# Thresholded attention and a gated MLP in one kernel: MLP jobs three steps sooner, one more threshold on ScalarE in five pairs, another order of the tail

## The chip, the core and the metric

The kernel runs on one core of one Trainium2 chip, as one launch. The metric is the device time in microseconds; the kernel before took 480.41 us as the median of three runs (479.06 to 481.51). Engines are named as the profile names them: PE is TensorE's matmul, PEld its weight load, DVE VectorE, ACT ScalarE, POOL GpSimd, SP the engine whose queue issues most DMAs. "L586" is line 586 of the kernel before.

## What is computed

Attention over 8 batches of 8 heads, 576 rows of 64, in which only scores within tau of a row's maximum count, and then a gated MLP with a spatial product over the 576 rows:

```python
scores = (1 / np.sqrt(64)) * np.matmul(q, k.transpose(0, 1, 3, 2))      # q, k, v: (8, 8, 576, 64)
thresh = np.max(scores, axis=-1, keepdims=True) - tau                   # tau = 0.02
scores = np.where(scores >= thresh, scores, -1e9)
attn = np.exp(scores - np.max(scores, axis=-1, keepdims=True))
attn = attn / (np.sum(attn, axis=-1, keepdims=True) + 1e-9)
x = np.matmul(attn, v)                           # heads side by side: (8, 576, 512)
h = np.maximum(x @ w_in, 0)                      # w_in: (512, 1024)
u, v = h[..., :512], h[..., 512:]
v_n = (v - mean(v)) / np.sqrt(var(v) + 1e-6)     # over the last axis
v_s = np.einsum('ts,bsd->btd', w_spatial, v_n) + b_spatial[None, :, None]
out = (u * v_s) @ w_out                          # (8, 576, 512)
```

## The kernel before, in words

**Pairs, chunks, steps.** Two heads make a pair i, of which there are 32, four to a batch. The 576 rows of a pair are cut into chunks c = 0 to 3 of 128 rows; the 64 rows left over of an even pair and of the odd pair after it make one chunk 4, which is done at the start of the odd pair. So an even pair has the steps 0, 1, 2, 3 and an odd one 4, 0, 1, 2, 3: 144 steps g = 0 to 143, nine to two pairs, eighteen to a batch. The order of all queues is written out by hand: each step writes its instructions in turn, and each engine runs its own in that order.

**One step** (`step`, L574). PE multiplies the scores of both heads into a tile s of three PSUM banks (`scores`, L545 for the last 64 columns, L550 for the first 512); there are two such tiles, so the scores of step g+2 wait until the exponentials of step g have read theirs. DVE takes the maximum (L586). On most chunks ACT then computes e = exp(s - max), one instruction a head (L609), and DVE, one step later in `mask` (L558), sets what is below exp(-tau) to nothing and writes p in bf16 (L567, a SCALAR_TENSOR_TENSOR over 1152 columns). On the chunks for which `on_act` is true the threshold is ACT's: DVE turns the negative maximum into tau - max (L590), ACT runs Prelu with a slope of 1e30 below zero (L603, in the place of L609) and one Exp over 1152 columns that writes p (L605); `mask` then has no DVE work. Before, these are chunks 2 and 4. After chunk 1 and chunk 3, `mask` issues on SP a DMA transpose of two chunks of p into pT (L571), after chunk 4 one of the rest (L562).

**Jobs in a step.** `fs` lists what a step does beside its own scores: the transposes of the next pair's q and k on PE with copies by ACT (qk_main at chunks 0 and 2, qk_rem at chunk 1), the product with v (pv, L289 and L294; its divide is DVE's, L301 and L303), and the jobs of the MLP. The list is sorted so that jobs that ACT evicts come first and jobs that DVE evicts after them, the products of the left-over rows (pv_rest) last. The first two are put before the maximum; ACT's evictions of these go ahead of the step's exponentials. Further jobs are put after the exponentials, and their ACT evictions are held until the next step. All jobs but the scores rotate through two PSUM banks (tiles f), so the third job of a step waits for the eviction of the first.

**MLP jobs.** For each batch b there are five v jobs (moe_v: x times the right half of w_in, L418; ACT's Relu L428, two steps later its Square L442, and a chain on POOL that writes the normalised vn, L436 to L448; the fifth, L403 and L406, has the rest rows and the last rows of the output of the batch before), five u jobs (moe_u, L460 and L465, ACT's Relu L475 or L477), five s jobs (moe_s, the spatial product, L490 and L495, whose gating product with u is DVE's, L504 or L507), and four o jobs (moe_o, L519, ACT's copy L524 and an output DMA). They are placed by three names: batch b's round begins at step LAG + 18 b, the letters of ORDER are put one to a step from there on, and s and o belong to the batch before. With 19 letters the last o shares its step with the first letter of the next round. Jobs whose step would lie beyond 143 go into `last` and are run in the tail.

**Other work with a step number.** `x_jobs` transposes x on PE for the first seven pairs; later pairs use DMA transposes. `ws_pe` transposes w_spatial on PE, five jobs. `chores` holds loads of the weights on SP and casts on POOL. The loads of q, k and v go through `sends`, one a step, behind `mask`. POOL reorders q, k and v for the pairs to come (shape_qk at chunk 2, shape_v at chunk 0).

**The head and the tail.** The first pair's transposes go to the banks of the score tiles (`first`). After step 143 the score tiles are given up and the other banks are six more; `run` writes jobs one after the other: those in `last`, the last products with v, the transposes of x on PE (x_pe), the s jobs of batch 6, and then `last_gmlp` for batch 7, which starts with its v products (L643).

Of the kernel before, what the change touches and what calls it, by code (L numbers as in the profile page):

```python
# [17 lines left out]
def kernel(  # L18
# [21 lines left out]
    NPAIR = B * H // 2  # L40
# [267 lines left out]
    def pv(i, part):  # L308

        b, hp = divmod(i, HP)  # L310
        hold = {}

        def mm():
            t = hold["t"] = bank()
            for k in range(2):
                weigh(t, 130 * k, pts[i, part][:, k], v_ring[i % 4])

        def ev():
            if part == 0:
                xns[i] = xp.tile([P, 4, P], BF16, name="xn")  # L320
            xn = xns[i]
            divide(hold["t"], [(slice(0, P), 0, 4,
                                xn[:, 2 * part:2 * part + 2, :].rearrange(
                                    "p c (h d) -> p (c h) d", h=2))])
            if part == 1:
                if hp == 0:
                    xts[b] = xtp.tile([P, 4, 640], BF16, name="xT")
                if i in x_on_pe:
                    return
                sends.append(lambda: nc.sync.dma_start_transpose(  # L330
                    out=xts[b][:, hp, 0:512].rearrange("p (c s) -> p c s", s=P),
                    in_=xn.rearrange("p c d -> p (c d)")))
        return "dve", mm, ev
# [217 lines left out]
                                 rhs=qks[n][hs, 1, 0:512], start=True, stop=True)  # L551
        return view(s, 0, [[960, 2], [1, S]])

    def on_act(c):

        return c in (2, 4)

    def mask():  # L558
        i, c, e = unmasked.pop()
        if c == 4:  # L560
            dst = pts[i // 2] = ptr_ring[i // 2 % 2]
            nc.sync.dma_start_transpose(out=dst, in_=pr_ring[i // 2 % 2])  # L562
            return
        pt = p_ring[2 * (i % 2) + c // 2]
        if not on_act(c):
            ef = e.rearrange("p h s -> p (h s)")
            nc.vector.scalar_tensor_tensor(out=pt[:, c % 2, :], in0=ef, scalar=ctau, in1=ef,  # L567
                                           op0=ALU.is_ge, op1=ALU.mult)
        if c % 2:
            dst = pts[i, c // 2] = ptp.tile([P, 2, 9, P], BF16, name="pT")  # L570
            nc.sync.dma_start_transpose(out=dst.rearrange("p c b s -> p (c b) s"),  # L571
                                        in_=pt.rearrange("p c s -> p (c s)"))

    def step(i, c, fs):  # L574

        s = scores(i, c)
        while held:
            held.pop(0)()


        for kind, mm, ev in fs[:2]:
            mm()
            if kind == "act":
                ev()
        nm = small.tile([P, 2], F32, name="negm")
        nc.vector.tensor_reduce(out=nm, in_=s, axis=AX.X, op=ALU.max, negate=True)  # L586

        by = scale if c == 4 else 1.0
        if on_act(c):
            nc.vector.tensor_scalar(out=nm, in0=nm, scalar1=by, scalar2=float(tau),  # L590
                                    op0=ALU.mult, op1=ALU.add)
        for kind, mm, ev in fs[:2]:
            if kind == "dve":
                ev()
        due = [f for n, f in later if n <= 0]
        later[:] = [(n - 1, f) for n, f in later if n > 0]
        for f in due:
            f()
        e = ep.tile([P, 2, S], F32, name="e")
        if on_act(c):  # L600

            for h in range(2):
                nc.scalar.activation(out=e[:, h, :], in_=s[:, h, :], func=ACT.Prelu,  # L603
                                     bias=nm[:, h:h + 1], scale=by, alpha=1e30)
            nc.scalar.activation(out=pr_ring[i // 2 % 2] if c == 4 else p_ring[2 * (i % 2) + c // 2][:, c % 2],  # L605
                                 in_=e.rearrange("p h s -> p (h s)"), func=ACT.Exp)
        else:
            for h in range(2):
                nc.scalar.activation(out=e[:, h, :], in_=s[:, h, :], func=ACT.Exp,  # L609
                                     bias=nm[:, h:h + 1])  # L610
        ready = sends[:]
        sends.clear()
        if unmasked:
            mask()
        for f in ready:
            f()
        unmasked.append((i, c, e))
        for kind, mm, ev in fs[2:]:
            mm()
            if kind == "dve":  # L620
                ev()
            else:
                held.append(ev)
# [115 lines left out]
    chores[13] = (load_w_in, 3)  # L739
    for gs_, f in (((4, 5, 6, 17), shape_w_in),  # L740
                   ((20, 25, 30), load_ws), ((24, 26, 29, 31, 34), shape_ws),
                   ((36, 41, 46, 51), load_w_o), ((39, 44, 49, 54), shape_w_o)):
        chores.update({g: (f, j) for j, g in enumerate(gs_)})

    LAG = 26
    ORDER = "vsvsvsvssuvuouououo"
    jobs, last = {}, []
    for b in range(B):  # L750
        n = dict.fromkeys("vuso", 0)
# [10 lines left out]
    Z = B - 1  # L762
# [1 line left out]
    for g, j in x_jobs:  # L764
        jobs.setdefault(g, []).append((x_pe, j))
    for j in range(5):
        jobs.setdefault((29, 33, 34, 42, 44)[j], []).append((ws_pe, j))
    with tc.manual_schedule():
        for w in (0, 1):
            for f in load(0, 1, w, (nc.sync, nc.scalar)[w]):  # L770
                f()
        make_identity(nc, identf)
        clear()
        nc.vector.memset(ntau, -float(tau))
        nc.vector.memset(mhalf, -0.5)
        nc.scalar.activation(out=ctau, in_=ntau, func=ACT.Exp)
        nc.vector.tensor_copy(out=identb, in_=identf)
        for w in (0, 1):
            for f in load(1, 1, w):
                f()  # L780
        for f in load(0, 2, 2):
            f()
        for j in range(3):
            load_w_in(j)
        for _ in range(14):
            nc.tensor.transpose(out=ps_f.tile([P, 512], F32, name="f")[:, 0:P], in_=identf,
                                identity=identf)
        shape_first()
        first()
        shape_qk(1)  # L790
        queue = []
        for g, (i, c) in enumerate(steps):
            if c == 2 and i + 2 < NPAIR:
                shape_qk(i + 2)
            if c == 0:
                shape_v(i)
            if c == 0 and i % 2 and i + 3 < NPAIR or g == 0:
                for w in range(3):
                    queue.extend(load(i + (3 if g else 2), 2, w))
            if g in chores:  # L800
                chores[g][0](chores[g][1])
            fs, small_ones = [], []
            if i + 1 < NPAIR and c < 3:
                fs.append(qk_rem(i + 1) if c == 1 else qk_main(i + 1, c // 2))
            if i and c == (2 if i % 2 else 3):
                fs.append(pv(i - 1, 0))
            if i > 1 and c == 4:
                fs.append(pv(i - 2, 1))
            if i % 2 and c == 3:
                fs.append(pv(i - 1, 1))  # L810
            if i % 2 and i > 1 and c == 1:
                small_ones = [pv_rest(i // 2 - 1)]
                fs += small_ones
            fs += [f(*a) for f, *a in jobs.get(g, [])]
            fs.sort(key=lambda f: (f[0] == "dve", f in small_ones))
            sends += queue[:1 if g > 3 else 2]
            del queue[:1 if g > 3 else 2]
            step(i, c, fs)

        def run(*fs):  # L820
            for f in fs:
                f[1]()
                f[2]()
                for f in sends:
                    f()
                sends.clear()
        while held:
            held.pop(0)()
        mask()
        inner.close()  # L830
        wide.append(ctx.enter_context(tc.tile_pool(name="ps_t", bufs=6, space=PSUM,
                                                  reuse_waits="tile")))
        for _, f in later:
            f()
        last = [f(b, j) for f, b, j in last]
        run(last[0], pv_rest(NPAIR // 2 - 1), *last[1:3], x_pe(NPAIR - 2), *last[3:6],
            pv(NPAIR - 1, 0), *last[6:], pv(NPAIR - 1, 1), moe_s(Z - 1, 0), moe_s(Z - 1, 1),
            x_pe(NPAIR - 1, True), *[moe_s(Z - 1, j) for j in range(2, 5)])
        rest = last_gmlp(Z)
        next(rest)  # L840
        run(moe_u(Z, 0), moe_u(Z, 1))
        next(rest)
        run(*[moe_u(Z, j) for j in range(2, 5)], *[moe_o(Z - 1, j) for j in range(4)])
        next(rest)
        next(rest, None)
# [35 lines left out]
```

## Time and profile before, and how to read it

| what | us |
|---|---|
| median of three runs | 480.41 |
| the profiled execution | 480.41 |
| its span, first to last instruction | 478.6 |
| scores of step 5, 23, 45 start at | 19.27, 68.26, 134.53 |
| a round of 18 steps from step 45 to 135 | 55.24, 55.67, 55.35, 55.21, 55.21 |
| last maximum (step 143) starts at | 437.70 |
| v products of batch 7 (L643) start at | 452.82 |

| one instruction | count | mean us |
|---|---|---|
| L586 DVE maximum | 144 | 1.353 |
| L567 DVE threshold | 96 | 1.444 |
| L590 DVE tau - max | 48 | 0.305 (median 0.170) |
| L609 ACT Exp of one head | 192 | 0.741 |
| L603 ACT Prelu of one head | 96 | 0.738 |
| L605 ACT Exp to p, both heads | 48 | 1.165 |

The page gives for each engine the busy time and its share of the span. The table by stretch gives the same for a piece of the span: its bounds and length, then busy us and instructions of PE, PEld, DVE, ACT and POOL, TensorE's granted clock, the share of the DMA engines, and GB/s. The timeline lists start, duration, engine, line, operation, tiles, and in brackets how long the engine sat idle before and what released it. The chain that ended last is followed back from the last instruction, and shows start, duration and line. Instructions that follow each other on DVE and ACT overlap by some 0.08 us in their records, so I count from start to start where a sum matters.

### The profile page before, as it was taken

The page shows a single profiled execution, that of the slowest core. Times are in us where ns is not written, and L with a number is a line of the kernel's source. Part 1 is how long each engine was busy: PE and PEld are TensorE (multiplying, and loading weights), DVE is VectorE, ACT ScalarE, POOL GpSimd, SP SyncE. Part 2 cuts the span into 40 slices and gives each one's busy share as a digit, 9 for nine tenths or more (in the row PEclk, how much of TensorE's full clock was granted, in tenths as well). Part 3 has the DMA queues.
Part 4 walks back from the last instruction along what each step waited for, and adds up shares of the span by engine and source line. Part 5 has one row for each costly group of instructions (what it writes and reads, how often), then busy time and mean ns, then how long its engine had stood idle before and what let it go on. Part 6 is the DMA issues. An engine that isn't in the chain of part 4 may idle for free.

```text
span 478.6 us, 9894 instructions
## 1 busy us (share of the span) xinstructions
PE 448.3 (94%) x3664; PEld 238.3 (50%) x3664; DVE 418.0 (87%) x563; ACT 382.2 (80%) x666; POOL 229.1 (48%) x403
## 2 busy tenths in 40 slices
PE   7788888889899999999999999999999999999995
PEld 4344444454554555554555545555554545545542
DVE  4999999989889997999889898899889998898573
ACT  4778777998879798788979898798978889797251
POOL 3462544784337553474427652475436743253021
PEclk9899999999999999999999999999999999999999
DMA  7999999979999799898988999997996999766523
GB/s 225 255 185 199 223 236 197 214 159 204 179 191 194 172 212 223 189 170 183 192 197 202 182 200 191 223 190 156 222 227 170 195 173 218 138 113 120 149 82 117
DMA packets 231120, 89.38 MB, mean 187 GB/s; under 512 B 200608, under 2 KB 225312, under 8 KB 231072
## 3 DMA queue, kind: packets, MB, share of 16 engines
q1 hardware_dynamic: 230416, 87.86, 87.2%
q8 instruction: 29, 0.48, 0.4%
q0 software_dynamic: 160, 0.52, 0.3%
q10 hardware_dynamic: 496, 0.36, 0.2%
q14 instruction: 19, 0.16, 0.1%
HBM read 33.31 MB, written 9.44 MB: 89 GB/s over the span
## 4 chain that ended last, share of the span: by engine, by line
PE 48%; DVE 23%; ACT 19%; issue 6%; DMA 2%; SPq 1%; POOL 0%; POOLq 0%; ACTq 0%; DVEq 0%
PE s L550 14%; DVE negm L586 10%; DVE p L567 8%; PE f L245 5%; ACT e L609 5%; PE s L545 4%; ACT e L603 4%; PE f L294 4%; PE f L519 4%; PE f L460 3%; ACT p L605 2%; ACT vrel L428 2%; PE f L490 2%; PE f L289 2%; ACT sq L442 1%
## 5 line engine op out<-in xcount | busy, mean ns | idle before, releaser
L586 DVE TENSOR_REDUCE negm<-s 128x2 f32<-128x1152 f32 x144 | 194.8, 1353 | 26.1 <-PE s L550 25.3
L550 PE MATMUL s<-qkT 64*128 64x512 f32 (+1 forms) x640 | 162.9, 639 | 0.0
L567 DVE SCALAR_TENSOR_TENSOR p<-e,ctau 128x1152 bf16<-128x1152 f32 x96 | 138.6, 1444 | 1.3 <-ACT e L609 1.2
L609 ACT ACTIVATE e<-s,negm 128x576 f32<-128x576 f32 x192 | 131.8, 741 | 7.1 <-DVE negm L586 6.8
L603 ACT ACTIVATE e<-s,negm 128x576 f32<-128x576 f32 x96 | 65.9, 738 | 20.9 <-DVE negm L590 11.6
L545 PE MATMUL s<-kd,qkT 128*128 128x128 f32 (+1 forms) x320 | 64.4, 304 | 15.6 <-ACT e L609 10.5
L268 POOL COPY kd<-qkT 64x64 f32<-64x64 f32 x62 | 31.7, 512 | 91.2 <-ACT qkT L263 89.4
L545 PEld LDWEIGHTS s<-kd,qkT 128*128 128x128 f32 (+1 forms) x320 | 44.4, 180 | 34.7 <-ACT e L609 20.2
L550 PEld LDWEIGHTS s<-qkT 64*128 64x128 f32 (+1 forms) x640 | 42.1, 174 | 18.3 <-issue 3.0
L436 POOL TENSOR_SCALAR nmean<-sm 128x1 f32<-128x1 f32 (+1 forms) x35 | 15.3, 437 | 69.7 <-ACT vrel L428 64.3
L294 PEld LDWEIGHTS <-pT 128*128 128x128 bf16 x1024 | 41.8, 97 | 7.3 <-issue 4.8
L294 PE MATMUL f<-v,pT 128*128 128x65 bf16 x992 | 44.9, 194 | 0.0
L136 POOL COPY qn<-ql 128x640 f32<-128x640 f32 x31 | 34.7, 1120 | 21.2 <-DMA ql<-in_k_dram 15.1
L605 ACT ACTIVATE p<-e 128x1152 bf16<-128x1152 f32 x32 | 37.3, 1165 | 1.0
L252 ACT COPY qkT<-f 128x512 f32<-128x512 f32 x31 | 18.2, 587 | 16.4 <-PE f L245 16.4
L490 PE MATMUL f<-wsT,vn 128*128 128x512 bf16 x125 | 31.1, 379 | 0.0
L448 POOL TENSOR_SCALAR vn<-vrel,rs,nm 128x512 bf16<-128x512 f32 (+1 forms) x34 | 28.7, 844 | 3.7
L289 PE MATMUL f<-v,pT 128*128 128x130 bf16 x124 | 27.2, 219 | 3.5 <-ACT qkT L252 1.6
L460 PE MATMUL f<-xT,w_in 128*128 128x512 bf16 x112 | 28.7, 380 | 0.9 <-DVE xn L303 0.8
L418 PE MATMUL f<-w_in,xT 128*128 128x512 bf16 x112 | 28.8, 380 | 0.0
L303 DVE TENSOR_TENSOR xn<-f,r 128x256 bf16<-128x256 f32 x62 | 26.3, 425 | 2.1
L428 ACT ACTIVATE vrel<-f 128x512 f32<-128x512 f32 (+1 forms) x34 | 20.1, 592 | 7.6 <-PE f L418 5.2
(165 smaller groups left out, 638.7 us busy)
## 6 DMA issues: line engine op xcount, KB each, us to landing
vl<-in_v_dram SPq DMA_DIRECT2D x16, 512.0 KB, 4.4
ql<-in_q_dram SPq DMA_DIRECT2D x15, 512.0 KB, 4.6
kl<-in_k_dram SPq DMA_DIRECT2D x15, 512.0 KB, 4.5
out_dram<-o SPq DMA_DIRECT2D x20, 256.0 KB, 3.4
uT<-in_moe_w_in_dram SPq DMA_DIRECT2D x3, 512.0 KB, 6.6
uT<-in_moe_w_spatial_dram SPq DMA_DIRECT2D x2, 576.0 KB, 5.0
vl<-in_v_dram SPq DMA_DIRECT2D x16, 64.0 KB, 4.1
pT<-p SPq DMA_TRANSPOSE x64, 5.5
```

Of the source, the lines that this page charges most:

```text
L136: nc.gpsimd.tensor_copy(out=t, in_=ld_ring[i // 2 % 2][w][:, 2 * (i % 2):2 * (i % 2) + 2].rearrange("p h c d -> p c h d"))
L289: nc.tensor.matmul(out=t[:, at:at + 130], lhsT=pt[:, 4, :], rhs=vt[:, 4:6, :].rearrange("p b d -> p (b d)"), start=True, stop=False)
L294: nc.tensor.matmul(out=t[:, at + 65 * h:at + 65 * h + 65], lhsT=pt[:, 5 * h + j, :], rhs=vt[:, 6 * h + j, :], start=False, stop=(h == 1 an ...
L460: nc.tensor.matmul(out=t, lhsT=w_in[:, m, f * P:(f + 1) * P], rhs=xts[b][:, m, 0:512], start=(m == 0), stop=(m == 3))
L490: nc.tensor.matmul(out=t, lhsT=vn[:, c, f * P:(f + 1) * P], rhs=wsT[:, c, 0:512], start=(c == 0), stop=(c == 4))
L545: nc.tensor.matmul(out=view(s[rows], 512, [[448, 2], [1, 64]]), lhsT=qks[n][:, 0, m], rhs=kd_ring[n % 2], start=True, stop=True)
L550: nc.tensor.matmul(out=s[rows, 1024 * h:1024 * h + 512], lhsT=qks[n][hs, 0, m], rhs=qks[n][hs, 1, 0:512], start=True, stop=True)
L567: nc.vector.scalar_tensor_tensor(out=pt[:, c % 2, :], in0=ef, scalar=ctau, in1=ef, op0=ALU.is_ge, op1=ALU.mult)
L586: nc.vector.tensor_reduce(out=nm, in_=s, axis=AX.X, op=ALU.max, negate=True)
L603: nc.scalar.activation(out=e[:, h, :], in_=s[:, h, :], func=ACT.Prelu, bias=nm[:, h:h + 1], scale=by, alpha=1e30)
L605: nc.scalar.activation(out=pr_ring[i // 2 % 2] if c == 4 else p_ring[2 * (i % 2) + c // 2][:, c % 2], in_=e.rearrange("p h s -> p (h s)"), ...
L609: nc.scalar.activation(out=e[:, h, :], in_=s[:, h, :], func=ACT.Exp, bias=nm[:, h:h + 1])
```

## The change

Four edits. `on_act` also holds for chunk 0 of pairs 1 to 5 (steps 5, 9, 14, 18 and 23). LAG goes from 26 to 23 and ORDER changes: the v jobs keep their steps, but for the fifth, which is two sooner; the u jobs come three or four steps sooner, the s jobs four to six and the o jobs three. The transposes of w_spatial are spread over other steps, and w_out is loaded and cast one to four steps sooner. In the tail `last` now holds six jobs instead of nine, and two of batch 6's s jobs go between the two last products with v, a third before x_pe.

```diff
-    def on_act(c):
-
-        return c in (2, 4)
+    def on_act(i, c):
+
+        return c in (2, 4) or c == 0 and 0 < i < 6
...
-                   ((36, 41, 46, 51), load_w_o), ((39, 44, 49, 54), shape_w_o)):
+                   ((35, 39, 43, 47), load_w_o), ((38, 42, 46, 50), shape_w_o)):
...
-    LAG = 26
-    ORDER = "vsvsvsvssuvuouououo"
+    LAG = 23
+    ORDER = "sssvsvsvuvuvouououo"
...
-        jobs.setdefault((29, 33, 34, 42, 44)[j], []).append((ws_pe, j))
+        jobs.setdefault((27, 29, 35, 37, 39)[j], []).append((ws_pe, j))
...
         run(last[0], pv_rest(NPAIR // 2 - 1), *last[1:3], x_pe(NPAIR - 2), *last[3:6],
-            pv(NPAIR - 1, 0), *last[6:], pv(NPAIR - 1, 1), moe_s(Z - 1, 0), moe_s(Z - 1, 1),
-            x_pe(NPAIR - 1, True), *[moe_s(Z - 1, j) for j in range(2, 5)])
+            pv(NPAIR - 1, 0), moe_s(Z - 1, 0), moe_s(Z - 1, 1), pv(NPAIR - 1, 1),
+            moe_s(Z - 1, 2), x_pe(NPAIR - 1, True), moe_s(Z - 1, 3), moe_s(Z - 1, 4))
+        assert len(last) == 6, len(last)
```

The calls of `on_act` pass the pair as well. Instructions change in number only by the five thresholds: five L567 fewer, five L590 and five L605 more, ten L603 in the place of ten L609.

## The prediction

> **What bounds the kernel now.** I read the page's busy shares first, then the same engines by stretch, then the waits, then the chain at the end. The profiled execution took 480.41 us for a span of 478.6 us. That is also the median of the three runs, so I work in its times and need no correction between the two; 1.8 us lie outside the span.
>
> ```profile
> PE 448.3 (94%) x3664; PEld 238.3 (50%) x3664; DVE 418.0 (87%) x563; ACT 382.2 (80%) x666; POOL 229.1 (48%) x403
> ```
>
> One share for the whole span says little, because the kernel has a head, a steady middle and a tail. The table by stretch (columns: us, then busy us of each engine) parts them. Steps are counted by the starts of the L545 matmuls: step 14 starts at 43.15, 23 at 68.26, 45 at 134.53, and from there each round of 18 steps takes 55.2 to 55.7 us, up to step 135 at 411.21.
>
> ```profile
> 45.50:70.60 25.10, 20.14 (x178) 10.91 (x177) 24.70 (x31) 19.08 (x30) 9.67 (x14) 1.00 1.00 209
> 70.60:96.10 25.50, 22.60 (x190) 12.01 (x189) 24.10 (x30) 22.30 (x41) 16.11 (x28) 1.00 1.08 207
> 96.10:123.20 27.10, 24.65 (x208) 13.40 (x207) 24.19 (x30) 24.70 (x45) 17.50 (x33) 1.00 0.91 185
> 300.80:356.00 55.20, 54.48 (x453) 28.82 (x450) 49.36 (x63) 47.42 (x85) 28.82 (x49) 1.00 0.92 196
> ```
>
> ```profile
> 437.70:474.00 36.30, 36.02 (x296) 18.37 (x292) 23.00 (x54) 16.19 (x31) 5.00 (x6) 1.00 0.40 107
> ```
>
> The reader is to see three regimes. Before gMLP begins (first row) DVE is busy 24.70 of 25.10 us; PE has 5 us to spare, ACT 6. In a steady round (fourth row) it is PE: 54.48 of 55.20, and its gaps add to 0.7 us. In the tail PE is busy 36.02 of 36.30. So work taken off DVE pays in the head, work taken off PE pays in the tail, and in the middle only the order can matter. The timeline of DVE in the head carries the first claim; no row has an idle mark:
>
> ```profile
> 68.64 0.17 DVE L590 TENSOR_SCALAR negm<-negm 128x2 f32<-128x2 f32 x1
> 68.72 0.17 DVE L301 RECIPROCAL r<-f 128x4 f32<-128x4 f32 x1
> 68.93 0.42 DVE L303 TENSOR_TENSOR xn<-f,r 128x256 bf16<-128x256 f32 x1
> 69.27 1.41 DVE L567 SCALAR_TENSOR_TENSOR p<-e,ctau 128x1152 bf16<-128x1152 f32 x1
> 70.60 2.76 DVE L586 TENSOR_REDUCE negm<-s 128x2 f32<-128x1152 f32 x2
> ```
>
> And the chain that ended last, at the seam of loop and tail, goes over from DVE to PE:
>
> ```profile
> 436.46 1.33 DVE p L567
> 437.78 1.27 DVE negm L586
> 439.05 0.10 DVE r L301
> ...
> 439.66 1.04 PE f L460 x4
> 440.69 0.86 PE t L519 x4
> ```
>
> **Term 1, the threshold in pairs 1 to 5 (steps 5, 9, 14, 18, 23).** Each loses one L567 on DVE, from start to start 69.27 to 70.60 = 1.33 us, and gains one L590, 68.64 to 68.72 = 0.08 (its mean is 0.305, its worst 1.12 where GpSimd copies beside it). DVE saves 5 x 1.25 = 6.25 us. ACT gains one L605 of 1.165 us each, some 1.1 from start to start; the two Prelu replace two Exp at 738 against 741 ns. For the row 45.50:70.60, with two such pairs, DVE falls from 24.70 to 22.2 and ACT rises from 19.08 to 21.3, PE stays at 20.1: DVE stays the longest, so up to 2.5 us per nine steps may go. What is late next: Prelu now waits for reduction and L590 where Exp waited for the reduction alone; the exponentials of the next step queue behind L605 on ACT, and PE's scores two steps on wait for them. SP is the other: between 45.3 and 70.6 its issues add to 23.6 us, the pT transposes among them at 2.7 to 5.0 us each, with both rings of loads between them. If those durations are fixed, nine steps can't go below 23.6, a gain of 1.5 instead of 2.5. Pair 1 saves less: its L567 at 25.59 follows 0.98 us in which DVE waited for PE. Bounds 0 to -6.25; I take **-4.0**, nearer to the DVE row, because SP's shortest pT issue (2.7) shows that the long ones stretch with the queue.
>
> The Trainium skill, ScalarE: Activation LUTs, section Table sets, says that a switch between functions of different sets costs a table load, about 2.66 us. Were Prelu and Exp in different sets, five pairs would pay two switches each, an estimate of 27 us more, and the sum would be 501 us. Page part 5 by shape has one load in the whole execution, although chunks 2 and 4 alternate the two functions 48 times, so I charge nothing:
>
> ```profile
> L776 ACT ACT_TABLE_LOAD x1 | 1.3, 1283 | 2.0 <-issue 2.0
> ```
>
> **Term 2, the tail.** With LAG 23 the last round fits 13 jobs into the loop, not 10: the fifth v job, one u and one o leave the tail. There they cost PE 0.9 (four L403/L406 pairs, 437.77 to 438.66), 0.87 and 0.86 (439.66 to 440.69 to 441.56 in the chain): -2.6. The loop's last five steps lose three s jobs too: two L504 and one L507, 0.6 + 0.6 + 0.33 us on DVE, which the chain shows binding there until 439.66. ACT gets a u, the v job and its copies instead, and has a 2.5 us idle stretch before 435.69 to take them. I count half of 1.5: -0.7. The order of the tail: pv(31,1) needs the transpose that was issued at 441.97 and landed at 446.55, while pv(31,1) ran at 447.02. Counting PE forward from the last scores (435.33) with three jobs fewer and s0, s1 put ahead of it, it comes up at 445.3; with the loop's end 0.7 to 1.5 earlier the landing comes to 445.1 to 445.9. The two meet, so the wait is 0 to 0.6. The divide behind it (0.6 on DVE) lies beside s2 (1.08 on PE). Each job that moves takes its output DMA along (one for o, one for the fifth v, 0.54 us of SP) and the v job its chain on GpSimd, which is busy 12.5 of the loop's last 29 us; both have room. Bounds: -4.1 with all of 1.5, and -1.0 where the wait is 0.6 and ACT's new work holds the loop's end back by 1; I take **-3.3**.
>
> **Term 3, what the loop takes in.** Up to step 44 it now also runs s0, s1, s2 of batch 0 (steps 41 to 43): 3 x 1.08 us on PE, 3 x 0.6 on DVE. PE's gaps between 68 and 134 add to 6.6 us, so a part lies in them; PE's scores, evictions and weights' transposes of steps 27 to 43 come to some 47.4 us of PE, 46 of DVE, 48 of ACT for 51 elapsed. Bounds 0 to +3.3, I take **+1.3**. The w_o loads and casts come 1 to 4 steps sooner, with the same three steps between load and cast; the cast's 2.3 us of waiting is on GpSimd with nothing due. The transposes of w_spatial at steps 27 and 29 read chunks that GpSimd cast by 71.9 and 78.2, before those steps. Both nothing; if that cover went, one PE stall of about the cast's 1.1 us.
>
> The Trainium skill, Trace Analysis, section Identifying the Most-Contended Engine, holds that matmul busy time is no measure and that the weight loads' share is: 50% here, so PE would have room and term 3 would be 0. The gaps in a steady round (0.7 of 55.2 us) speak against it, as far as order and clock go; I keep +1.3.
>
> **Term 4, the steady rounds.** Five to six of them do the same work in another order. I added each step's work by the starts in the timeline. PE: scores 1.36, qk_main 0.59, qk_rem 0.26, pv 0.62, v, u and o 0.87, s 1.08, the fifth s 0.6, the fifth v 0.97. DVE: reduction 1.30, L567 1.36, L590 0.12, divide 0.55 (0.70 for pv_rest), s 0.6, the fifth 0.33. ACT: two exponentials 1.36, L605 1.12, a copy 0.5, v 0.65 (1.15 for the fifth), its square 0.78. DVE exceeded PE most at an odd pair's chunks 1 and 2 with s3 and s4: 3.96 + 3.69 against 3.32 + 3.17, +1.16 us; those steps took 3.67 and 3.36, so 0.54 was lost. Now s1 and s2 stand on such steps: 3.96 + 3.96 against 3.32 + 3.65, +0.95. On ACT the worst was an even chunk 2 with a copy for o and a square, 4.26 against PE's 2.82; now it is an odd chunk 2 with the fifth v job, 4.91 against 3.54: +1.4 both times. The end of a round had v and o together; now o and s share a step in which DVE has no mask. Bounds per round: -0.7 (all PE gaps) to +0.9 (old friction stays and the new adds as much); for six, -4 to +5.4. I take **0**.
>
> **Sum.** -4.0 - 3.3 + 1.3 + 0 = -6.0: 480.4 - 6.0 = **474.4 us**.
>
> **Rivals.** *SP and the loads set the head.* Then DVE's relief turns into PE waits for pT (already 3.6 us in the head) and GpSimd waits for k (11.8 us): term 1 is 0, and the three s jobs cost all of 3.3: 480.4 - 2.6 + 3.3 - 0.7 = 480.4; with half of each, 479. For it: SP is issuing 23.6 of 25.25 us. Against: nothing in DVE's stream waits on it now. *The three s jobs in a row bind every round.* On the odd pair's chunks 0, 1, 2 the gating products and two masks meet on DVE, and the two f banks must be freed by ACT for a third job in each of three steps. The nearest price is the old pair of steps, 0.54 us over PE's work; if the new stretch costs 1.6 a round, six rounds are +9.6 and the sum is -6.0 + 9.6 = +3.6: **484.0 us**. It decides from 1.0 us a round. Against: o3 and s0 come where DVE has 2 us of work for 3.9 of PE. *More than forecast*: term 1 whole and the rounds' gaps closed: -6.25 - 4.1 + 0.5 - 3 = 467.6.
>
> **Numbers.** The forecast's case (470 to 477.9) 0.62, more 0.08, the first rival 0.16, the third-job rival 0.14. What a measurement of this kernel can tell from no change is about 0.5%, 2.4 us. Faster than 478.0: 0.62 + 0.08 + 0.02 of the first rival = 0.72; within: 0.14 of the first rival and 0.01 of the other = 0.15; slower than 482.8: 0.13. The range takes the forecast and the first rival and a part of the others: 468.5 to 482.0.
>
> **What would show it.** Steps 5 to 23 should fall from 49.0 us to about 45.8 (four of the five pairs); if DVE's rows get idle marks before L586 and SP's do not shrink, the first rival holds. The last batch's v products (L643) should start near 446.9 instead of 452.8, since every term lies before them, and from there to the end it should stay 25.8 us. A round should stay within 54.5 to 56.1; above 56.2 the s jobs bind. PE waits for pT at pv(31,1) above 0.6 us would spoil term 2.

## The result and the profile after

The kernel after takes 493.16 us (median of four runs, 491.82 to 493.98) against 479.74 (four, 478.19 to 481.51: the three of the prediction and one more): 1.0276 times, 95% interval 1.0229 to 1.0322. It is slower, where 474.4 was forecast. Medians here and below are of all runs; the ratios leave out executions in a slower state, which were three of ten in one experiment (the changed kernel without the Square) and none elsewhere. The profiled execution took 493.98 us for a span of 492.17, 13.57 more than the span of before. All stretches below are taken from it, from start to start of the same step's L545.

| stretch | before | after | difference |
|---|---|---|---|
| start to step 5 | 19.27 | 19.45 | +0.18 |
| steps 5 to 23 (head) | 48.98 | 47.23 | -1.75 |
| steps 23 to 27 | 11.42 | 11.10 | -0.32 |
| steps 27 to 45 (first round) | 54.85 | 59.92 | +5.07 |
| steps 45 to 135 (five rounds) | 276.68 | 287.94 | +11.26 |
| steps 135 to 143 | 22.67 | 23.13 | +0.46 |
| step 143 to the end (tail) | 44.72 | 43.39 | -1.33 |

The head and the tail gained as meant, but less. The rounds, costed at nothing, took 2.25 us each, and the first round 5.07. Each line is one profile against one profile, which matters for the head and the first round (see the part on why). The page's shares hardly show the loss: the busy times of PE, DVE and ACT are within 6 us of those before, POOL's is 9 lower, and the span has grown by 13.57.

```profile
PE 449.8 (91%) x3664; PEld 239.2 (49%) x3664; DVE 414.5 (84%) x563; ACT 387.7 (79%) x673; POOL 220.4 (45%) x407
```

The chain that ended last has moved: 39% of the span is PE's in it and 28% ACT's, where before it was 48% and 19%.

```profile
PE 39%; ACT 28%; DVE 16%; issue 10%; DMA 5%; POOL 0%; SPq 0%; POOLq 0%; ACTq 0%
```

The table by stretch answers to the rows of before (length, then busy us of PE, PEld, DVE, ACT, POOL, clock, DMA share, GB/s). The first row holds the same nine steps, from maximum to maximum, as the first of before; the second is a steady round; the third goes from step 143 to the v products of the last batch.

```profile
45.10:68.76 23.66, 19.76 (x175) 10.59 (x175) 21.13 (x30) 21.12 (x32) 7.65 (x13) 1.00 1.03 226
295.07:352.66 57.59, 54.63 (x455) 28.96 (x451) 50.38 (x64) 47.38 (x84) 26.91 (x49) 1.00 0.87 184
448.78:466.36 17.58, 15.41 (x172) 8.88 (x170) 11.66 (x24) 9.32 (x19) 4.84 (x9) 1.00 0.64 146
```

In the nine head steps DVE's work fell by 3.6 us, the time by only 1.44: DVE now has 2.5 us to spare and binds no more. In a round PE's work is the same (54.63 against 54.48), and its idle time is 2.96 us against 0.73: **nearly the whole loss of a round is PE waiting**. In the tail PE idles 2.17 of 17.58.

Where PE waits in a round is read from its timeline (start, duration, engine, line, tiles, and in brackets the idle time and its releaser). Of 57.59 us, these are the waits of over 0.2:

```profile
298.81 1.24 PE L490 MATMUL f<-wsT,vn 128*128 128x512 bf16 x5 [0.77 <-ACT qkT L250]
305.88 0.22 PE L289 MATMUL f<-v,pT 128*128 128x130 bf16 x1 [0.65 <-DVE xr L303]
318.80 0.49 PE L545 MATMUL s<-kd,qkT 128*128 128x128 f32 x2 [0.29 <-ACT e L609]
331.16 0.22 PE L289 MATMUL f<-v,ptr 128*128 128x130 bf16 x1 [0.72 <-ACT qkT L263]
344.37 0.49 PE L545 MATMUL s<-kd,qkT 128*128 128x128 f32 x2 [0.23 <-ACT e L609]
```

The round of before has three waits, at the second place, the fourth and the last:

```profile
296.31 0.22 PE L289 MATMUL f<-v,pT 128*128 128x130 bf16 x1 [0.21 <-ACT qkT L252]
321.25 0.22 PE L289 MATMUL f<-v,ptr 128*128 128x130 bf16 x1 [0.27 <-ACT qkT L263]
334.11 0.49 PE L545 MATMUL s<-kd,qkT 128*128 128x128 f32 x2 [0.18 <-ACT e L609]
```

The longest new one is ahead of the third job, s0, of the odd pair's step 0 (step 95 here), and the timeline of that step, with ACT's rows, says why:

```profile
296.52 0.66 PE L245 MATMUL f<-identf,qn 128*128 128x128 f32 x4
297.02 1.03 PE L519 MATMUL f<-w_o,gT 128*128 128x512 bf16 x4
297.11 1.16 ACT L605 ACTIVATE pr<-e 128x1152 bf16<-128x1152 f32 x1
298.18 0.58 ACT L250 ACTIVATE qkT<-f 128x512 f32<-128x512 f32 x1
298.81 1.24 PE L490 MATMUL f<-wsT,vn 128*128 128x512 bf16 x5 [0.77 <-ACT qkT L250]
300.09 0.69 DVE L504 TENSOR_TENSOR gT<-f,uT 128x512 bf16<-128x512 f32 x1 [1.28 <-PE f L490]
```

qk_main's product (L245) and o3's (L519) fill the two f banks. The copy that empties the first (L250) queues on ACT behind chunk 4's Exp of both heads (L605), which runs until 298.27. So s0 starts at 298.81, where PE was free at 298.05. Before, this step had two jobs, qk_main and a u, and none had to wait for a bank. The steps of the round that differ most, in us, in both kernels and in two experiments below ("o with v" and "Exp put off there"):

| step (pair, chunk) | jobs after | before | after | o with v | Exp put off there |
|---|---|---|---|---|---|
| 94 (odd, 4) | u4, pv | 3.00 | 2.49 | 2.49 | 2.49 |
| 95 (odd, 0) | qk_main, o3, s0 | 2.81 | 4.81 | 3.03 | 3.89 |
| 96 (odd, 1) | qk_rem, s1, pv_rest | 3.02 | 3.24 | 3.24 | 3.24 |
| 97 (odd, 2) | qk_main, s2, pv | 3.40 | 4.45 | 4.16 | 4.16 |
| 98 (odd, 3) | v0 | 3.87 | 2.90 | 3.76 | 2.89 |
| 105 (odd, 1) | qk_rem, u, pv_rest | 3.68 | 3.90 | 3.91 | 3.91 |
| 106 (odd, 2) | qk_main, v, pv | 3.36 | 3.66 | 3.66 | 3.65 |

### The profile page after: what moved, and what is told of

It reads as the page before. It is cut to its first block, busy times and chain, and to the rows that moved or that the text cites. A ratio compares the mean times of both kernels' runs of the same rounds, so it can differ in the third digit from the quotient of the medians.

```text
span 492.2 us, 9915 instructions
## 1 busy us (share of the span) xinstructions
PE 449.8 (91%) x3664; PEld 239.2 (49%) x3664; DVE 414.5 (84%) x563; ACT 387.7 (79%) x673; POOL 220.4 (45%) x407
## 4 chain that ended last, share of the span: by engine, by line
PE 39%; ACT 28%; DVE 16%; issue 10%; DMA 5%; POOL 0%; SPq 0%; POOLq 0%; ACTq 0%
PE s L550 12%; DVE negm L586 9%; ACT e L609 7%; ACT e L603 7%; DVE p L567 5%; PE f L490 4%; DMA pT<-p 4%; PE s L545 4%; ACT sq L442 4%; PE f L294 3%; PE f L245 3%; ACT p L605 2%; ACT vrel L428 2%; ACT qkT L250 2%; ACT pr L605 2%
## 5 line engine op out<-in xcount | busy, mean ns | idle before, releaser
L586 DVE TENSOR_REDUCE negm<-s 128x2 f32<-128x1152 f32 x144 | 195.0, 1354 | 38.7 <-PE s L550 38.3
L550 PE MATMUL s<-qkT 64*128 64x512 f32 (+1 forms) x640 | 162.8, 642 | 0.0
L567 DVE SCALAR_TENSOR_TENSOR p<-e,ctau 128x1152 bf16<-128x1152 f32 x91 | 135.8, 1493 | 3.0 <-ACT e L609 2.9
L609 ACT ACTIVATE e<-s,negm 128x576 f32<-128x576 f32 x182 | 124.8, 741 | 11.6 <-DVE negm L586 11.4
L603 ACT ACTIVATE e<-s,negm 128x576 f32<-128x576 f32 x106 | 72.9, 743 | 21.8 <-DVE r L301 10.4
L545 PE MATMUL s<-kd,qkT 128*128 128x128 f32 (+1 forms) x320 | 63.9, 304 | 16.2 <-ACT e L609 10.0
L268 POOL COPY kd<-qkT 64x64 f32<-64x64 f32 x62 | 15.6, 251 | 101.9 <-ACT qkT L263 100.2
L545 PEld LDWEIGHTS s<-kd,qkT 128*128 128x128 f32 (+1 forms) x320 | 44.9, 179 | 32.9 <-ACT e L609 18.7
L550 PEld LDWEIGHTS s<-qkT 64*128 64x128 f32 (+1 forms) x640 | 42.0, 175 | 18.4 <-issue 2.9
L436 POOL TENSOR_SCALAR nmean<-sm 128x1 f32<-128x1 f32 (+1 forms) x35 | 17.7, 505 | 69.2 <-ACT vrel L428 69.2
L448 POOL TENSOR_SCALAR vn<-vrel,rs,nm 128x512 bf16<-128x512 f32 (+1 forms) x35 | 43.4, 1240 | 3.8
L605 ACT ACTIVATE p<-e 128x1152 bf16<-128x1152 f32 x37 | 43.1, 1164 | 1.2
L156 POOL CAST v<-vl 128x640 bf16<-128x640 f32 x32 | 36.4, 1137 | 0.6 <-DMA vl<-in_v_dram 0.6
L490 PE MATMUL f<-wsT,vn 128*128 128x512 bf16 x130 | 32.1, 378 | 3.8 <-ACT qkT L250 3.8
L136 POOL COPY qn<-ql 128x640 f32<-128x640 f32 x31 | 29.3, 945 | 13.1 <-DMA ql<-in_k_dram 11.5
L460 PE MATMUL f<-xT,w_in 128*128 128x512 bf16 x104 | 26.8, 380 | 0.0
```

The lines of the kernel that those rows point to most:

```text
L136: nc.gpsimd.tensor_copy(out=t, in_=ld_ring[i // 2 % 2][w][:, 2 * (i % 2):2 * (i % 2) + 2].rearrange("p h c d -> p c h d"))
L156: nc.gpsimd.tensor_copy(out=bass.AP(v_ring[i % 4].tensor, v_ring[i % 4].offset, [v_ring[i % 4].ap[0], [6 * (D + 1), 2], [D + 1, 5], [1, D] ...
L448: nc.gpsimd.tensor_scalar(out=dst, in0=vrel[:n], scalar1=rs[:n], scalar2=nm[:n], op0=ALU.mult, op1=ALU.add)
L490: nc.tensor.matmul(out=t, lhsT=vn[:, c, f * P:(f + 1) * P], rhs=wsT[:, c, 0:512], start=(c == 0), stop=(c == 4))
L545: nc.tensor.matmul(out=view(s[rows], 512, [[448, 2], [1, 64]]), lhsT=qks[n][:, 0, m], rhs=kd_ring[n % 2], start=True, stop=True)
L550: nc.tensor.matmul(out=s[rows, 1024 * h:1024 * h + 512], lhsT=qks[n][hs, 0, m], rhs=qks[n][hs, 1, 0:512], start=True, stop=True)
```

## The experiments

**The threshold alone.** The kernel before with the one edit of `on_act`.

```diff
-        return c in (2, 4)
+        return c in (2, 4) or c == 0 and 0 < i < 6
```

> The kernel before with only the threshold of chunk 0 in pairs 1 to 5 moved to ScalarE. Theory (the loss is the jobs': a step's third job waits for the bank that ScalarE frees late): this edit is innocent and brings what the changed kernel had gained by step 23, 1.8 us: about 478. Rival (the threshold edit disturbs the steps behind it, by ScalarE's longer queue or by SP): 480 or more.

It took 478.42 us against 479.27: 0.9974 [0.9958, 0.9991]. Of the versions that compute the same, this one alone is faster than the kernel before: by 0.9 us, which is little, but the interval leaves out 1.

**The jobs alone.** The kernel after without that edit.

```diff
-        return c in (2, 4) or c == 0 and 0 < i < 6
+        return c in (2, 4)
```

> The changed kernel with the threshold edit undone, everything else kept. Theory (the jobs cost it all): 493.2 + 1.8 = 495. Rival (the two edits harm each other, ScalarE being loaded by the threshold just before the MLP begins): well below 493, towards 485.

494.44 us, 1.0308 [1.0270, 1.0345]; a round takes 57.58 us. So the moved jobs, with the loads and the tail that go with them, cost all of the loss. The threshold pays about 1 us: 0.9 in the kernel before, and in the changed one 1.3 between two medians whose intervals overlap.

**The last o with the first v.** The kernel after, with only the last letter of ORDER put three steps later, to step 98 and its like; it takes the third job out of step 95.

```diff
-            g = LAG + PER * b + j
+            g = LAG + PER * b + (j if j < 18 else 21)
```

> The changed kernel with the last o job of each round three steps later, beside the first v job, where it was in the kernel before; so the step of the odd pair's chunk 0 has two jobs instead of three. Theory (third job waits for a bank): that step falls from 4.8 to about 3.0 us, the step that takes the o job rises from 2.9 to 3.87; 0.85 us a round, five rounds: about 489. Rival (the four steps from the odd pair's chunk 0 on hold more PE work than before, whatever the order): their sum stays, 492 to 493.5.

487.45 us, 1.0153 [1.0124, 1.0181]: 5.7 us below the kernel after, more than expected. A round takes 56.37. Step 95 falls by 1.78, step 97 by 0.29, and step 98 takes 0.86 back. The same stretch of PE, with no wait left ahead of s0:

```profile
293.76 0.66 PE L245 MATMUL f<-identf,qn 128*128 128x128 f32 x4
294.25 1.24 PE L490 MATMUL f<-wsT,vn 128*128 128x512 bf16 x5
295.33 0.39 PE L545 MATMUL s<-kd,qkT 128*128 128x128 f32 x2
```

This run alone doesn't tell the bank's wait from the mere number of jobs in the step. The next two keep the jobs and move ACT's instruction.

**Chunk 4's Exp put off, in all odd pairs.** L605 of chunk 4 is written behind the next step's copies instead of ahead of them.

(The operands are shortened to "..." here.)

```diff
+            def wide_exp():
-            nc.scalar.activation(out=pr_ring[...] if c == 4 else ..., func=ACT.Exp)
+                nc.scalar.activation(out=pr_ring[...] if c == 4 else ..., func=ACT.Exp)
+            if c == 4:
+                put_off.append(wide_exp)
+            else:
+                wide_exp()
...
+        while put_off:
+            put_off.pop(0)()
         nm = small
```

> The changed kernel with one instruction of ScalarE put off: chunk 4's Exp over 1152 columns goes behind the copies of the next step's first two jobs, in the place ahead of them. No job moves. Theory (PE's third job waits for the copy of the q transposes, which queues behind this Exp for 1.1 us): the step of the odd pair's chunk 0 falls from 4.8 to about 4.0, five rounds: about 489. Rival (DVE's gating products and masks, or PE's work, set these steps): within 1 us of 493.

492.76 us, 1.0273 [1.0236, 1.0310]: in the total the rival's number, a miss of 4 us for the theory. By steps, 95 fell from 4.81 to 3.89 as expected and 97 from 4.45 to 4.16, but step 105, of the other odd pair, rose from 3.90 to 4.73. There the Exp that was put off comes just ahead of the Square of a v job, and both now stand before L263, the copy whose bank pv_rest takes:

```profile
327.83 1.15 ACT L609 ACTIVATE pr<-e 128x1152 bf16<-128x1152 f32 x1
328.89 0.71 ACT L442 ACTIVATE sq<-vrel,nmean 128x512 bf16<-128x512 f32 x1
329.59 1.36 ACT L618 ACTIVATE e<-s,negm 128x576 f32<-128x576 f32 x2
330.84 0.27 ACT L263 COPY qkT<-f 128x128 f32<-128x128 f32 x1
331.16 0.22 PE L289 MATMUL f<-v,ptr 128*128 128x130 bf16 x1 [1.54 <-ACT qkT L263]
```

(In this kernel L609 is the Exp of both heads and L618 that of one.) The wait in front of pv_rest is 1.54 instead of 0.72. So the order on ACT decides at both places, with opposite signs.

**Put off only where the third job waits.** The same edit with one condition more, `if c == 4 and i > 8 and i % 4 == 1`.

> As the run with chunk 4's Exp put off, but only in every second odd pair, from pair 9 on: where o3 and s0 share the next step. Theory (bank behind that Exp; at the other odd pairs the put-off Exp itself cost 0.8 us): step 95 and its like 3.9 instead of 4.8, two steps on 4.16 instead of 4.45, nothing given back: 1.2 us in each of five rounds, about 487. Rival (what PE does not wait for there it waits for elsewhere): 492 or more.

487.73 us (486.26 to 491.33), 1.0181 [1.0131, 1.0230], with every round at 56.37 to 56.40. The jobs stand where the kernel after has them, and only one ACT instruction a round has moved: 5.4 us of the loss by the medians, 6.0 in the five rounds of the profile, come from that order. The copy now ends before the Exp begins, and PE doesn't wait:

```profile
295.97 0.60 ACT L250 ACTIVATE qkT<-f 128x512 f32<-128x512 f32 x1
296.64 1.24 PE L490 MATMUL f<-wsT,vn 128*128 128x512 bf16 x5
296.84 0.59 ACT L524 COPY o<-f 128x512 f32<-128x512 f32 x1 [0.27 <-PE f L519]
297.32 1.17 ACT L609 ACTIVATE pr<-e 128x1152 bf16<-128x1152 f32 x1
```

**x transposes apart from the u jobs.** In the first round the moved u0, u3 and u4 of batch 0 meet the x transposes of steps 31, 38 and 40. This kernel is the one after with the three elsewhere.

```diff
-(31, 4), (38, 5), (40, 6))
+(28, 4), (36, 5), (37, 6))
```

> The changed kernel with the transposes of x for pairs 4, 5 and 6 at steps 28, 36 and 37 in the place of 31, 38 and 40, where u0, u3 and u4 of batch 0 had come to meet them. Theory (a third job waits for a bank wherever ScalarE frees the first job's late): steps 31 and 38 to 40, 16.2 us in the changed kernel against 11.1 before, give back 2 to 4 us: 489 to 491. Rival (these steps hold more work than before, and its place does not matter): 492 to 493.5.

491.92 us, 1.0275 [1.0237, 1.0314], 1.2 below the kernel after, and within its runs; the expected 489 to 491 is missed. By its profile the first round takes 56.80 us instead of 59.92, but its head was 1.0 longer. Its two longest waits there, 1.07 and 1.29, are still behind copies of the x transposes (L374); the kernel after has 1.76, 0.84 and 0.82. How the kernel after loses there, in its PE timeline of steps 39 and 40:

```profile
116.51 0.45 PE L388 MATMUL f<-identb,wsb 128*128 128x128 bf16 x5
118.72 0.22 PE L289 MATMUL f<-v,pT 128*128 128x130 bf16 x1 [1.76 <-ACT xT L374]
...
119.43 0.70 PE L545 MATMUL s<-kd,qkT 128*64 128x128 f32 x4
120.06 1.99 PE L550 MATMUL s<-qkT 64*64 64x512 f32 x8
```

The 1.76 us are again a job (pv) that waits for a bank whose copy queues on ACT, behind an Exp: the bank is that of the x transposes, the third job of the step before. A transpose of w_spatial (L388), which the change also moved, shares that step; no run moved it alone. After the wait the matmuls ran at half the clock for 3.4 us: L550 took 1.99 where the jobs alone, after a wait of 1.67 at the same place, had 1.09. Step 40 took 4.66 in the kernel after and 3.12 there, so 1.5 us of the 5.07 are the clock's and not directly the order's.

**Another order of the tail.** The kernel after with s2 put ahead of the last product with v, and s3 ahead of x_pe.

```diff
-pv(NPAIR - 1, 0), moe_s(Z - 1, 0), moe_s(Z - 1, 1), pv(NPAIR - 1, 1), moe_s(Z - 1, 2), x_pe(NPAIR - 1, True), moe_s(Z - 1, 3), moe_s(Z - 1, 4)
+pv(NPAIR - 1, 0), moe_s(Z - 1, 0), moe_s(Z - 1, 1), moe_s(Z - 1, 2), pv(NPAIR - 1, 1), moe_s(Z - 1, 3), x_pe(NPAIR - 1, True), moe_s(Z - 1, 4)
```

> The changed kernel with a third s job put ahead of the last product with v in the tail, s0 s1 s2 pv s3 x_pe s4 in the place of s0 s1 pv s2 x_pe s3 s4. Theory (PE waits 1.5 us there for the last transpose of p, which lands behind two output DMAs that the moved jobs brought along): 1.1 to 1.5 us less, about 491.8. Rival (the divide behind that product then comes late for x_pe, and the wait only moves): 493.

492.46 us, 1.0268 [1.0233, 1.0303]. The medians part by 0.7, too little to stand alone, and not the 1.1 to 1.5 expected; in the profile the tail from step 143 is 1.20 shorter (42.19), and the wait for the transpose falls from 1.52 to 0.31 us. The wait of the kernel after, and the two output DMAs ahead of the transpose on SP:

```profile
454.21 0.55 SPq L433 DMA_DIRECT2D out_dram<-o  x1
454.85 0.55 SPq L528 DMA_DIRECT2D out_dram<-o  x1
456.24 2.77 SPq L571 DMA_TRANSPOSE pT<-p  x1
...
462.71 0.23 PE L289 MATMUL t<-v,pT 128*128 128x130 bf16 x1 [1.52 <-DMA pT<-p]
```

**Three mends at once.** The kernel after with the edits of the last o, the x transposes and the tail.

> The changed kernel with three mends together: the last o job beside the first v job, the transposes of x at steps 28, 36, 37, the third s job ahead of the last product with v. If the three are independent: 487.4 - 3 - 1.4 = 483. Rival (the place of the u and s jobs in the round costs whatever is mended): it stays above before's 479.3 by some 1.2 us for each of five rounds, so 483 too, and 479 or less would refute that rival.

484.41 us, 1.0102 [1.0076, 1.0127]: 8.7 us back, and still slower than before. Its rounds stay at 56.4. Theory and rival both said 483, so this run doesn't choose between them.

**The rest of a round.** What do the last 1.1 us of a round wait for? Both kernels without the Square of the v jobs (0.78 us of ACT, five a round): the one with the last o moved, and the one before.

```diff
-                nc.scalar.activation(out=sq[:n], in_=vrel[:n], func=ACT.Square,
-                                     bias=nmean[:n], accum_out=ss[:n])
...
-in0=ss[:n], scalar1=1.0 / 512, scalar2=1e-6,
+in0=sm[:n], scalar1=1.0 / 512, scalar2=1e-6,
```

> The changed kernel with the last o job beside the first v job, and without ScalarE's Square of the v jobs (the normalisation takes the mean in place of the variance; some 0.8 us of ScalarE for each v job, 3.9 a round, are left out). It goes with the kernel before treated alike. Theory (what is left, 1.2 us a round, is ScalarE: with the u jobs and the fifth v job moved there it sets the steps from an even pair's chunk 1 to the odd pair's chunk 2): the round falls from 56.4 to about 55, 1.4 us, the whole to about 480. Rival (what is left is PE work moved into steps that PE sets): the round falls by no more than that of the kernel before does.

> The kernel before without ScalarE's Square of the v jobs (mean in place of the variance). The control for the run above. Theory (PE sets most of its round, ScalarE little): the round falls from 55.2 to 54.7 at most, the whole to 476 to 479. Rival: as much as in the changed kernel, 1.4 us a round, 471.

The first took 480.56 us (ten runs, 474.86 to 487.65), 0.9986 [0.9952, 1.0020], its five rounds 54.83, 55.69, 55.85, 55.80 and 55.87 instead of 56.37; the second 479.10, 0.9984 [0.9963, 1.0005], its rounds 55.3 on average as before. So in the steady rounds ACT's load binds the new order and not the old one, but they gain 0.8 us, about half of what was expected. That the total came out near the expected 480 is luck: 3.0 us of it are the first round (59.11, a stretch of half clock in it, to 56.08), where the kernel before gains 2.0 too. Where the rest of the steady gain went is seen in the waits of one round without the Square:

```profile
295.73 0.22 PE L289 MATMUL f<-v,pT 128*128 128x130 bf16 x1 [0.65 <-DVE xr L303]
315.53 0.23 PE L289 MATMUL f<-v,pT 128*128 128x130 bf16 x1 [0.73 <-DMA pT<-p]
```

The waits behind ACT (0.72 for L263, 0.29 and 0.23 for the exponentials) are gone, and two others have come or grown: for the divide on DVE (0.36 with the Square), and for the transposes of p.

## Why the prediction was wrong

**Term 4 (0, measured +11.3) is the step that failed.** It put each step's work on each engine together and compared the sums: for o3 and s0, DVE had 2 us of work for 3.9 of PE, so the step seemed safe. PE's work in it was indeed 3.9, and the step took 4.81. (Two of its DVE sums come out 0.03 lower from its own terms, 3.66 and 3.93, which changes nothing.) A sum can't show that a third job needs the first job's bank, that the copy which frees it has a fixed place on ACT, and that this place is behind an Exp of 1.16 us. The rival had the mechanism in its words ("the two f banks must be freed by ACT") and the price per round at 1.6; measured are 2.25, of which 1.2 go with this one wait (56.37 with the Exp moved or the job moved). The other 1.1 are waits as well: PE idles 1.91 us of a round of 56.36 with the last o moved, against 0.73 of 55.21 before. In both of these kernels PE comes sooner to places where ACT or DVE set the pace: 0.72 instead of 0.27 at pv_rest, 0.36 instead of 0.21 at step 97, 0.29 at scores that had waited for nothing. That ACT holds part of them is shown by the kernels without the Square, where these waits go and 0.8 of the 1.1 comes back. What holds the rest is open: no run gives it back, and no other order of the u and s jobs was tried.

**"Above 56.2 the s jobs bind"** was the right sign to look for: 57.6. Of the three steps in a row that the rival named, though, the second costs little (3.24 against 3.02); the bank wait is in the first.

**Term 3 (+1.3, measured +5.07, of which 1.5 the clock).** Two profiles with the same jobs in this round and the full clock throughout it (the jobs alone, and the other order of the tail) have 58.41 and 58.06: +3.2 to +3.6 over before, at or just above the upper bound of 3.3. With the x transposes elsewhere the round takes 56.80, +1.95. That is what is left of everything together: the three s jobs, the u jobs and the w_spatial transposes in their new places, and waits of its own; the three s jobs were not run alone. The other 1.3 to 1.6 are the collisions of u0, u3 and u4 with x transposes, which the prediction didn't see: it listed the moved jobs' work, but didn't lay the new letters beside `x_jobs`.

**Term 1 (-4.0, measured -1.75 in the profile, -0.9 and -1.3 in the medians).** The profile's number can't be taken as the size. The kernel before ran step 5 at half the clock, the kernel after did not (3.50 us against 2.08; step 6 gives 1.1 of it back):

```profile
19.46:22.88 3.42, 3.42 (x11) 1.69 (x11) 3.38 (x4) 2.46 (x3) 3.21 (x6) 0.50 0.90 202
```

From step 5 to step 27 the nine profiles of kernels with the five thresholds take 58.33 to 61.01 us, the three without 59.53 to 60.40. The size is that of the threshold alone: -0.9. DVE's relief was there in full (3.57 us in nine steps, where two thresholds were to give 2.5). What would be late next had been named, "PE's scores two steps on wait for them", but priced at only 2.25 of 6.25. Between 18 and 68 us DVE's maximum now waits for scores ten times, 5.4 us in all (total, times, longest), against 1.4 us before, up to 70 us (second line):

```profile
DVE negm L586 <- PE s L550: 5.4, 10, 1.8
DVE negm L586 <- PE s L550: 1.4, 2, 1.0
```

and one such wait, traced back along the timeline of ACT, PE and DVE:

```profile
44.81 1.16 ACT L605 ACTIVATE pr<-e 128x1152 bf16<-128x1152 f32 x1
45.88 0.58 ACT L250 ACTIVATE qkT<-f 128x512 f32<-128x512 f32 x1
46.36 0.58 ACT L374 COPY xT<-f 128x512 bf16<-128x512 bf16 x1
46.83 1.38 ACT L603 ACTIVATE e<-s,negm 128x576 f32<-128x576 f32 x2
48.26 0.49 PE L545 MATMUL s<-kd,qkT 128*128 128x128 f32 x2 [0.50 <-ACT e L603]
49.86 1.36 DVE L586 TENSOR_REDUCE negm<-s 128x2 f32<-128x1152 f32 x1 [1.23 <-PE s L550]
```

ACT works without a gap from 44.81 to 48.21; the scores wait for its Prelu, and the maximum for the scores. With 21.13 us of DVE and 21.12 of ACT in 23.66 neither is the longest alone: in this stretch the loop from maximum over exponentials to the scores two steps on is. The first rival put the limit on SP; its sign came (idle marks before L586), and so did the number for nine steps if SP's durations are fixed (1.5 gained, 1.44 here), but the profiles scatter by as much. SP's issues do fill these nine steps as before, but in the head PE's matmuls wait only 1.6 us for pT, 0.6 before. (The prediction's 3.6 us are 0.6 of matmuls and 3.0 of weight loads; on that count, up to 80 us, it is 5.6 now.) Whether SP would hold the head if ACT did not is open; it was not tried.

**Term 2 (-3.3, measured -1.33).** All of it lies before the last maximum: from step 143 to that, 2.48 instead of 3.82 us; from there to L643 15.10 against 15.12. The second stretch, after and before:

```profile
451.26:466.36 15.10, 12.93 (x158) 7.75 (x156) 9.25 (x20) 6.91 (x13) 3.85 (x8) 1.00 0.68 157
437.70:452.82 15.12, 15.04 (x161) 8.57 (x158) 9.26 (x20) 7.47 (x15) 0.85 (x1) 1.00 0.67 157
```

PE had 2.1 us less work in it (12.93 against 15.04 busy) and waited 2.17: 1.52 for the transpose, forecast at 0 to 0.6, and 0.65 for a bank that ACT's copy of o (L524) held. The prediction counted the moved jobs' output DMAs and found room; but two of them are now issued 1.4 and 2.0 us ahead of the transpose, which took 6.4 us from issue to landing instead of 4.6. That they are the reason is not shown: no run issued the transpose without them. The new order of the tail moves PE's work ahead of the wait, not the landing (6.3 us there). From L643 to the end it stays 25.8 us, as forecast.

**What held:** the mean durations of single instructions on PE and ACT, and on DVE within 4% (L567 1.493 against 1.444), except L590 (0.209 against 0.305); the free switch between Prelu and Exp (one table load in the whole execution again); and the weights' loads and casts at no cost: no PE wait in the first round is released by them.

## What to carry to other kernels

When jobs are moved in an order written by hand, don't add up the work of a step alone: for each job, write down whose bank it takes, which instruction frees that, and what stands ahead of that instruction on its engine. A kernel whose bound engine idles 1.3% of a round has at most that to gain there from another order, and this one lost 4%. And lay the new step numbers beside all other lists that carry step numbers.

## What was not expected of the hardware

A wait of 1.76 us on PE was followed by half the clock; after 1.67 us at the same place in another kernel (the jobs alone) the clock stayed. It is not a single case: steps 39 and 40 ran so, in part, in two more profiles (the last o with the first v, and the Exp put off there), and step 5 in ten of the twelve kernels. In the records of the clock each slow time is 3.41 us or twice that, but for the one at the very end, and starts a whole number of 3.41 us after the record's first entry: in the kernel after that entry is at 6.80, and 33 times 3.413 later is 119.44. Cut at these times, the kernel after (the clock is the eighth column):

```profile
116.03:119.44 3.41, 1.65 (x29) 1.00 (x25) 2.51 (x2) 3.38 (x6) 2.56 (x4) 1.00 0.87 208
119.44:122.86 3.42, 3.42 (x31) 1.48 (x30) 1.36 (x3) 1.10 (x2) 0.00 (x0) 0.50 0.93 175
```

and the jobs alone:

```profile
115.75:119.17 3.42, 2.59 (x18) 1.30 (x17) 3.26 (x4) 3.11 (x5) 2.66 (x3) 1.00 0.90 193
119.17:122.58 3.41, 2.57 (x46) 1.53 (x46) 1.13 (x4) 2.66 (x5) 1.24 (x3) 1.00 1.20 266
```

In the first the whole wait lies in one stretch, in which PE is busy for 1.65 of 3.41 us; in the second it is split between two, with 2.59 and 2.57. That fits, but it isn't a rule: with 1.63 and 1.74 busy, in the changed kernel without the Square and in the one with the Exp put off in all odd pairs, the clock stayed.

The Trainium skill, TensorE: Matmul & The Clock Gate, Part 1, ties half the clock to an idle window of about 3.4 us that runs freely; 1.76 us is half of that. The length of the slow stretch (3.41 us) and its place on a fixed grid agree with it, a wholly idle window doesn't: PE was busy for half of the one before.
